# Cosformer attention and squared-ReLU MLP: the sequence tails become one more batch in seven products, the squares get three half buffers, and the casts of v move to GpSimd

## The chip, the cores and the metric

The kernel runs on one core of a Trainium2 chip, in one launch. The metric is the device time of that core in microseconds (us). Of the kernel before there are three timed runs and one profiled execution.

## The reference

```python
def _attn_ref(q, k, v):                       # q, k, v: (8, 8, 576, 64) float32
    theta = np.pi / 2.0 * np.arange(S) / S    # S = 576
    def phi(x, c, s):
        r = np.maximum(x, 0.0)
        return np.concatenate([r * c, r * s], axis=-1)
    q_p, k_p = phi(q, cos_w, sin_w), phi(k, cos_w, sin_w)
    kv = np.einsum('bhsf,bhsd->bhfd', k_p, v)
    z = np.sum(k_p, axis=2)
    num = np.einsum('bhsf,bhfd->bhsd', q_p, kv)
    den = np.einsum('bhsf,bhf->bhs', q_p, z)[..., None] + 1e-06
    return (num / den).astype(np.float32)

def _moe_ref(x, w_in, w_out):                 # x: the attention's output as (4608, 512)
    r = np.maximum(x @ w_in, 0.0)             # w_in: (512, 2048)
    return ((r * r) @ w_out).astype(np.float32)   # w_out: (2048, 512)
```

## The kernel before, in words

**Tiling.** The unit of work is one of the eight batches, with 576 positions: 512 main positions and a tail of 64. For each batch there is an attention part (features of k and q, casts of v, the small products `kz` and `num`, the division, transposes) and an MLP part on 512 tokens: a first matmul (`x @ w_in`, ReLU, square into `gT`) and a second one (`gT @ w_out`). The tails of four batches together make one more block of 256 tokens: tails of batches 0 to 3, and of 4 to 7.

**Plain and seven products.** Batches 0 to 2 do the first matmul plainly (`declare_plain`, lines 712 to 742: 16 blocks of eight matmuls with 256 columns each). Batches 3 to 7 (`SEVEN`, line 259) use a scheme with seven block products in the place of eight (`declare_seven1`, lines 810 to 872): four rounds of seven products of four matmuls, that is 112 matmuls for 512 tokens where the plain form takes 128. The price is sums: four differences of x per batch on VectorE (`declare_x_sums`, line 796), three copies per round on ScalarE, and per round two `add_relu` (line 421) on VectorE. The second matmul uses seven products in batches 1 to 7 (`declare_pair`, line 922): per pair of 128-token tiles, four sums of `gT` into `gs1` to `gs4` on VectorE (line 936), then Q1 to Q7 with eight matmuls each.

**The tails.** `declare_tails` (lines 746 to 769) makes the first matmul of a block of tails plainly, as eight pieces of eight matmuls: 64 per block, 128 in all. Lines 1236 to 1240 place the pieces: those of block 0 in batches 3, 4 and 5 (3, 3 and 2 pieces), those of block 1 in batches 6 and 7 (3 and 5 pieces). The second matmul of a block is a pair of its own (pair 2) in the middle of batches 5 and 7. `gTt` holds the squares of a block.

**Squares.** `gT` (line 311) is one buffer for the squares of 512 tokens. A square of the next batch can only be written when both pairs of the running batch have read that part; in rounds 0 to 2 one VectorE instruction squares all 512 tokens of two row blocks (line 870), in round 3 there are two halves (line 865).

**Casts.** `declare_v` (line 520) casts v to bf16 into `vx`. `declare_att` (line 1031) gives these casts to ScalarE for batches 3 to 7, to either of ScalarE and VectorE for batches 1 and 2. `vx` has five buffers; the cast of the next batch takes the buffers that `kz` (line 535) of the batch before has read. The load of v of the batch after has one buffer and waits for the casts.

**The order of the work.** Nothing is left to a scheduler at run time. Every operation is declared with the engines that may do it, an assumed cost, and for TensorE a position; `Planner.plan` (line 128) puts them into one fixed order for each engine, and the table `SHIFTS` (line 21) moves single operations, by their number, in it. All engines run their lists in order and wait on semaphores. So a changed list of operations gives a new order on all engines. SyncE's queue carries the loads of batches 0 and 3 to 7, all DMA transposes and the stores of batches 1 to 7; GpSimd's queue carries the weights, the loads of batches 1 and 2 and the two stores of batch 0 (`st_name`, line 876).

Of the kernel before, what the change touches and what calls it, by code (L numbers as in the profile page):

```python
# [20 lines left out]
SHIFTS = """  # L21
23:9.5:ACT 37:-0.5 38:1.0 44:17.5:ACT 46:-1.0 53:-0.5 62:11.5 79:-2.0 85:-2.5 89:3.0 93:11.0
108:5.5 144:9.0 152:-2.0 157:9.5:ACT 191:-5.0 194:-1.0 202:-1.5 203:-3.5:ACT 204:2.0 210:3.0
238:2.5 241:2.5 243:5.0 249:-6.0 257:-4.0 260:-2.0 261:-6.0 270:2.5 271:3.5 287:-5.0 325:-2.0
335:-0.5 340:1.5 348:8.5 354:-7.0 364:-19.0 383:1.0 390:-3.5 392:1.0 417:-4.5 487:-5.0 492:1.5
516:-7.5 517:-5.5 530:39.0 533:25.5 546:9.0 563:5.5 565:12.5 573:-8.5 575:5.0 588:13.0 593:4.5
598:-2.0 611:-4.5 617:-5.5 636:-1.5 670:7.5 677:-2.0 690:1.0 698:0.0:DVE 702:22.5 703:-19.5
704:3.5:ACT 706:-4.0 715:2.0 731:-2.5 748:5.0 781:-4.5 783:-6.0 785:-7.0 787:-2.0 790:-1.0
794:-1.5 797:1.0 799:1.0 807:11.0 813:-5.5 817:-4.0 820:-7.0 822:-5.5 836:-3.5 850:-3.5
859:-34.0 860:-15.0 870:1.0 872:-4.0 884:12.0 890:49.0 893:17.0 906:5.5 907:23.5 911:3.0 917:3.0  # L30
936:-3.0 951:-12.5 957:-1.0 958:-1.5 963:-3.5 985:7.0 990:-4.0 998:3.5 1005:-4.5 1009:5.5
1023:-10.0 1024:-8.5 1030:-10.0 1041:-26.0:ACT 1042:-10.5 1133:-13.0 1143:1.5 1155:4.0 1157:3.0
1176:-4.5 1191:4.5 1209:5.5 1247:2.5 1306:-0.5
# [200 lines left out]
def kernel(  # L234
# [24 lines left out]
    SEVEN = range(3, B)  # L259

# [7 lines left out]
        "round": 3, "rs": 6, "rt": 2, "u": 6, "gTt": 1, "ysb": 2,  # L268
        "gs1": 1, "gs2": 1, "gs3": 1, "gs4": 1,
# [7 lines left out]
    def many(pool, shape, dt=BF16):  # L277
# [29 lines left out]
        "gTt": many("gTt", [HB, 4 * TAIL]),  # L307
        **{f"gs{n}": many(f"gs{n}", [HBH, P]) for n in range(1, 5)},
        "ysb": many("ysb", [2, DM], F32),
    }  # L310
    gT = big.tile([P, HB, MAIN], BF16, name="gT")
# [126 lines left out]
    plan = Planner(POOLS, 4.5, ("gs1", "gs2", "gs3", "gs4"), 1.0, SHIFTS)  # L438
# [3 lines left out]
    TAILN = {3: 3, 4: 3, 5: 2, 6: 3, 7: 5}  # L442
    g1_len = {b: (7 if b in SEVEN else 8) * 16 * T_MM + TAILN.get(b, 0) * PROD2 for b in range(B)}
    g2_len = {b: 7 * PROD2 * (3 if b in (5, 7) else 2) if b else 8 * 2 * PROD2 for b in range(B)}
    att_len = 2.4
    T1, T2, t = {}, {}, 16.4
    for b in range(B):
        T1[b], T2[b] = t, t + g1_len[b] + att_len / 2
        t = T2[b] + g2_len[b] + att_len / 2

    loaded, kpb, vxb, kvzb, qpb, qpTb, xb, xTb, xTtb = ({} for _ in range(9))
# [68 lines left out]
    def declare_v(b, j, engs):  # L520
        buf = cached(vxb, (b, j), "vx" if j < J else "vxt")
        n = 1 if j < J else 0.65
        cost = {"ACT": 0.52 * n, "DVE": 0.34 * n}

        def cast(eng):
            copy(eng, at(buf)[:, :, 0:D], piece("v", b, j))

        add({e: cost[e] for e in engs}, cast, r=[source("v", b, j)], w=[buf])

    def declare_kz(b, pos, engs=("ACT",)):  # L530
        ba, bb = plan.buf("F"), plan.buf("F")
        kvz = kvzb[b] = plan.buf("kvz")
        for j in range(NS):

            def kz(_, j=j):
# [18 lines left out]
                ("PE", T_MM65 * (2 if j < J else 1) * HH + 0.02),  # L554
# [50 lines left out]
    def declare_num(b, j, pos):  # L605
# [22 lines left out]
        add(("PE", T_MM65 * n * HH + 0.015), num, r=[qT, kvzb[b]], w=bks, pos=pos)  # L628
# [76 lines left out]
    def gkey(hb, half):  # L705
        return ("g", hb // 2, half)
# [5 lines left out]
    def declare_plain(b, hb, half, pos, split=False):  # L712
# [3 lines left out]
        for c in range(2) if split else (None,):  # L716
# [23 lines left out]
            lambda _: square(gT[:, hb : hb + 2, half * TP : (half + 1) * TP], at(rt)),  # L740
            r=[rt], w=[gkey(hb, half)],
        )

    gttb, turned = {}, {}

    def declare_tails(b, hb, pos):

        bk, rt = plan.buf("F"), plan.buf("rt")
        xT = xTt_of(b)
        gt = cached(gttb, b // 4, "gTt")  # L750

        def tails(_):
            for i in range(2):
                for kb in range(KB):
                    mm(
                        bank(bk)[:, i * TP : (i + 1) * TP].rearrange("p (m c) -> p m c", m=4),
                        w1_at(kb, hb + i),
                        at(xT)[:, :, kb % 2, kb // 2, :],
                        i == 0 and kb == 0,
                        kb == KB - 1,  # L760
                    )

        add(("PE", PROD2), tails, r=[(xT, m) for m in range(4)] + [("w1", hb // 4)], w=[bk], pos=pos)
        add(("ACT", 0.5), lambda _: relu(at(rt), bank(bk).rearrange("p (i c) -> p i c", i=2)), r=[bk], w=[rt])
        add(
            ("DVE", 0.34),
            lambda _: square(at(gt)[:, hb : hb + 2, :], at(rt)),
            r=[rt], w=[(gt, hb // 2)],
        )
# [26 lines left out]
    def declare_x_sums(b):  # L796
        buf = xsb[b] = plan.buf("xs")
        x0, x1 = xT_of(b, 0), xT_of(b, 1)
        a = lambda kk, half: at((x0, x1)[half])[:, kk * KB2 : (kk + 1) * KB2, :]
        t = lambda n: a(0, 1) if n == 3 else at(buf)[:, min(n, 3) - 1]  # L800
        xk = [[(x0, 0), (x0, 1)], [(x1, 0), (x1, 1)]]
        for n, ops, reads in (
            (1, lambda: (a(0, 1), a(0, 0)), xk[0] + xk[1]),
            (2, lambda: (a(1, 1), t(1)), xk[1] + [(buf, 1)]),
            (3, lambda: (a(1, 1), a(0, 1)), xk[1]),
            (4, lambda: (a(1, 0), t(2)), xk[0] + [(buf, 2)]),
        ):
            add(("DVE", 0.34), lambda _, n=n, ops=ops: sub(t(n), *ops()), r=reads, w=[(buf, n)] + (xk[1] if n == 3 else []))

    def declare_seven1(b, r, t):  # L810
# [4 lines left out]
        xs, x0, x1 = xsb[b], xT_of(b, 0), xT_of(b, 1)  # L815
        xk = [[(x0, 0), (x0, 1)], [(x1, 0), (x1, 1)]]
        X = lambda kk, half: at((x0, x1)[half])[:, kk * KB2 : (kk + 1) * KB2, :]
        Tn = lambda n: X(0, 1) if n == 3 else at(xs)[:, min(n, 3) - 1]
        halves = lambda ap: ap.rearrange("p (i c) -> p i c", i=2)
        block = lambda i, j: at(rows[i])[:, :, j * TP : (j + 1) * TP]  # L820
        last = r == 3

        def product(name, off, acc, w, x, first, reads):
            def seven(_):
                for i in range(2):
                    for kb in range(KB2):
                        mm(
                            bank(acc)[:, i * TP : (i + 1) * TP],
                            w()[:, kb, i * P : (i + 1) * P],
                            x()[:, kb, :],  # L830
# [20 lines left out]
            ("DVE", 0.63), lambda _: add_relu(block(1, 1), halves(bank(E)), halves(at(u3))),  # L851
# [4 lines left out]
            ("DVE", 0.63), lambda _: add_relu(block(0, 1), halves(bank(E)), halves(at(u2))),  # L856
            r=[E, u2], w=[(rows[0], 1)],
        )
        for i in range(2):
            hb = i * HBH + 2 * r  # L860
            if last:
                for j in range(2):
                    add(
                        ("DVE", 0.34),
                        lambda _, i=i, j=j, hb=hb: square(gT[:, hb : hb + 2, j * TP : (j + 1) * TP], block(i, j)),
                        r=[(rows[i], j), turn], w=[gkey(hb, j)],
                    )
            else:
                add(
                    ("DVE", 0.6), lambda _, i=i, hb=hb: square(gT[:, hb : hb + 2, :], at(rows[i])),  # L870
                    r=[(rows[i], 0), (rows[i], 1), turn], w=[gkey(hb, 0), gkey(hb, 1)],
# [4 lines left out]
    def st_name(b):  # L876
        return "SP" if b >= 1 else "POOL"

    def st_eng(b):
        return nc.sync if b >= 1 else nc.gpsimd  # L880
# [24 lines left out]
    def four(b):  # L905
        return 0 if b < 7 else 1

    def g_at(b, pair, i, j):
        if pair == 2:
# [432 lines left out]
```

## Time and profile before

| what | value |
|---|---|
| timed runs | 276.74, 278.27, 279.21 us (median 278.27) |
| profiled execution: time, span | 276.82 us, 274.8 us |
| TensorE matmul busy | 267.9 us (98% of the span), 2845 matmuls |
| VectorE, ScalarE, GpSimd busy | 218.9, 194.9, 21.6 us |
| first wait for `w_in` after which TensorE runs without long gaps | until 22.19 us |
| last matmul starts, the span ends | 271.06 us, 274.8 us |

A page of the profile has the busy time of each engine, a strip of 40 slices (tenths of a slice that an engine was busy), the chain of work that ended last, and the costliest groups of instructions. Further answers of the trace are lists in order of time and tables of busy time by stretch. A matmul's recorded duration [...]overlaps with the next; the time from one start to the next is what it costs when TensorE is full. The same goes, less strongly, for VectorE and ScalarE.

### The profile page before, as it was taken

How to read it: one execution, taken by the hardware profiler on the slowest of the kernel's cores; microseconds unless marked ns; L12 is line 12 of the kernel's file. 1: busy time of each engine (PE TensorE's matmuls, PEld its weight loads, DVE VectorE, ACT ScalarE, POOL GpSimd, SP SyncE). 2: the span in 40 equal slices, each digit the busy share in tenths (PEclk: the TensorE clock that was granted, in tenths of full speed). 3: DMA queues.
4: the chain of work that ended last, by engine and by line, in shares of the span. 5: the costliest groups of instructions: out<-in, count | busy, mean ns of one | idle time of the engine just before them, and what ended most of it. 6: DMA issues, size and time to landing. Idle time of an engine off the chain costs nothing.

```text
span 274.8 us, 7115 instructions
## 1 busy us (share of the span) xinstructions
PE 267.9 (98%) x2845; PEld 227.6 (83%) x2845; DVE 218.9 (80%) x515; ACT 194.9 (71%) x391; POOL 21.6 (8%) x38
## 2 busy tenths in 40 slices
PE   8979999999999999999999999999999999999994
PEld 3668856789988988888888898988988888888884
DVE  1789996997694989699968999799968798279652
ACT  3876982997895598589957994699735954684522
POOL 1453544010000000000000000000000000000000
PEclk9999999999999999999999999999999999999999
DMA  7999999969979998899299955996198301200025
GB/s 217 321 205 290 296 283 365 219 218 225 361 160 186 281 334 156 224 347 221 81 164 308 259 181 102 265 338 217 35 205 170 91 2 44 95 16 2 1 79 153
DMA packets 81840, 53.01 MB, mean 193 GB/s; under 512 B 53584, under 2 KB 77648, under 8 KB 81808
## 3 DMA queue, kind: packets, MB, share of 16 engines
q1 hardware_dynamic: 75136, 40.12, 58.4%
q0 software_dynamic: 6528, 12.32, 17.1%
q8 instruction: 22, 0.36, 0.5%
q10 hardware_dynamic: 144, 0.13, 0.1%
q14 instruction: 10, 0.08, 0.1%
HBM read 36.70 MB, written 9.44 MB: 168 GB/s over the span
## 4 chain that ended last, share of the span: by engine, by line
PE 80%; DMA 8%; DVE 7%; issue 1%; SPq 1%; POOL 1%; ACT 1%; DVEq 0%
PE banks L430 79%; DMA w1sb<-in_moe_w_in_dram 4%; DMA qpT<-qp 2%; DMA vt<-in_v_dram 2%; DVE rs L422 2%; DVE gT L419 2%; DVE gs L427 2%; PE banks L591 1%; DVE x L639 1%; POOL w1sb L373 1%; SPq L366 0%; PE banks L682 0%; DVE qp L408 0%; DVE kp L408 0%; SPq L358 0%
## 5 line engine op out<-in xcount | busy, mean ns | idle before, releaser
L430 PEld LDWEIGHTS <-w1sb 128*128 128x128 bf16 x784 | 73.0, 98 | 10.4 <-DMA w1sb<-in_moe_w_in_dram 1.4
L430 PE MATMUL banks<-xT,w1sb 128*128 128x256 bf16 (+1 forms) x576 | 68.4, 267 | 1.0 <-DMA w1sb<-in_moe_w_in_dram 1.0
L430 PEld LDWEIGHTS <-gs 128*128 128x128 bf16 x512 | 49.0, 98 | 5.9 <-DVE gs L427 0.2
L416 ACT ACTIVATE rt<-banks 128x512 bf16<-128x512 f32 x64 | 37.2, 600 | 14.9 <-PE banks L430 9.3
L430 PEld LDWEIGHTS <-gT 128*128 128x128 bf16 x400 | 38.0, 98 | 9.0
L430 PE MATMUL banks<-w2sb,gT 128*128 128x256 bf16 (+1 forms) x288 | 44.2, 296 | 0.0
L430 PEld LDWEIGHTS <-w1s 128*128 128x128 bf16 x320 | 30.7, 98 | 3.7
L430 PE MATMUL banks<-w2sb,gs 128*128 128x256 bf16 x256 | 33.0, 273 | 0.0
L430 PE MATMUL banks<-w2s,gs 128*128 128x256 bf16 x256 | 32.2, 273 | 0.0
L422 DVE CUSTOM_DVE_ANT_0 rs<-banks,sums 128x512 bf16<-128x512 f32 x40 | 27.0, 684 | 4.5 <-ACT sums L847 3.1
L419 DVE TENSOR_TENSOR gT<-rs 128x1024 bf16<-128x1024 bf16 (+1 forms) x50 | 27.7, 579 | 1.8 <-ACT rs L416 1.0
L416 ACT ACTIVATE rs<-banks 128x512 bf16<-128x512 f32 x40 | 23.6, 604 | 3.1 <-PE banks L430 2.9
L430 PE MATMUL banks<-xs,w1s 128*128 128x256 bf16 x160 | 23.0, 273 | 0.0
L430 PE MATMUL banks<-xT,w1s 128*128 128x256 bf16 x160 | 22.9, 273 | 0.0
L419 DVE TENSOR_TENSOR gT<-rt 128x512 bf16<-128x512 bf16 x48 | 19.2, 418 | 4.5 <-ACT rt L416 4.3
L427 DVE TENSOR_TENSOR ysb<-banks,sums 128x256 f32<-128x256 f32 x32 | 13.4, 418 | 11.2 <-PE banks L430 7.3
L406 ACT ACTIVATE qp<-q,sin_col 128x512 bf16<-128x512 f32 x31 | 22.1, 738 | 0.1
L639 DVE TENSOR_TENSOR x<-banks,den 128x512 bf16<-128x512 f32 x30 | 20.7, 691 | 1.0
L406 ACT ACTIVATE kp<-k,sin_col 128x512 bf16<-128x512 f32 x30 | 21.2, 734 | 0.0
L427 DVE TENSOR_TENSOR gs<-gT 128x1024 bf16<-128x1024 bf16 x28 | 19.2, 686 | 1.1 <-PE banks L430 0.7
L413 ACT CAST vx<-v 128x512 bf16<-128x512 f32 x26 | 16.2, 636 | 0.9 <-DMA v<-in_v_dram 0.9
L637 DVE TENSOR_SCALAR den<-banks 128x8 f32<-128x8 f32 (+1 forms) x38 | 6.0, 159 | 12.5 <-PE banks L430 12.3
(106 smaller groups left out, 364.0 us busy)
## 6 DMA issues: line engine op xcount, KB each, us to landing
out_dram<-ysb SPq DMA_DIRECT2D x13, 512.0 KB, 3.5
k<-in_k_dram SPq DMA_DIRECT2D x6, 1024.0 KB, 6.4
v<-in_v_dram SPq DMA_DIRECT2D x5, 1024.0 KB, 7.9
q<-in_q_dram SPq DMA_DIRECT2D x5, 1024.0 KB, 9.3
w1sb<-in_moe_w_in_dram POOLq DMA_DIRECT2D x4, 512.0 KB, 10.5
q<-in_q_dram POOLq DMA_DIRECT2D x2, 1024.0 KB, 11.2
w2sb<-in_moe_w_out_dram POOLq DMA_DIRECT2D x4, 512.0 KB, 11.6
k<-in_k_dram POOLq DMA_DIRECT2D x2, 1024.0 KB, 11.3
```

The lines of the kernel that those rows point to most:

```text
L373: nc.gpsimd.dma_start(out=w1sb[:, :, f0:f1], in_=moe_w_in[:, f0:f1].rearrange("(kb p) f -> p kb f", p=P),)
L406: nc.scalar.activation(out=dst, in_=src, func=ACTF.Relu, scale=col)
L413: (nc.scalar.copy if eng == "ACT" else nc.vector.tensor_copy)(out=out, in_=in_)
L416: nc.scalar.activation(out=out, in_=in_, func=ACTF.Relu)
L419: nc.vector.tensor_tensor(out=out, in0=in_, in1=in_, op=ALU.mult)
L422: nc.vector._custom_dve(TENSOR_ADD_SAT, out=out, in0=in0, in1=in1, s0=float("inf"), s1=0.0)
L427: nc.vector.tensor_tensor(out=out, in0=in0, in1=in1, op=op)
L430: nc.tensor.matmul(out=out, lhsT=lhsT, rhs=rhs, start=start, stop=stop, skip_group_check=True)
L591: nc.tensor.transpose(t[:, h, :], qp_at(b, j)[:, h, :], ident[:, :])
L637: nc.vector.tensor_single_scalar(out=d, in_=n4[:, :, :, D], scalar=EPS, op=ALU.add)
L639: nc.vector.tensor_tensor(out=x_at(b, j).rearrange("p (b k) (l d) -> p b k l d", b=n, l=2), in0=n4[:, :, :, 0:D].rearrange("p b (k l) d -> ...
```

## The change

The tails of all eight batches become one more batch of 512 tokens, called `ENDS`, behind batch 6 and ahead of batch 7. Its first matmul is made in seven products, with the two blocks of tails as its two halves, so it has x sums, round copies and `add_relu` like the others; its second matmul is two pairs. `declare_tails`, `gTt` and the pairs 2 are gone. The squares go into three half buffers of 256 tokens (pool `gT`), which `claim` hands out in turn, so that the next batch can write into the third half and into the first one that comes free. The first product rounds are placed 3 to 6 us ahead (`LEAD`), among the second matmul of the batch before. The casts of v of batches 2 to 7 go to GpSimd as `tensor_scalar` (multiply by 1 twice). The cosine features of q may go to ScalarE or VectorE. The two stores of batch 0 go from GpSimd's to SyncE's queue. Assumed costs and `SHIFTS` are new, and with them the order on every engine.

```diff
+    ENDS = B
+    STAGES = [*range(B - 1), ENDS, B - 1]
...
-        "round": 3, "rs": 6, "rt": 2, "u": 6, "gTt": 1, "ysb": 2,
-        "gs1": 1, "gs2": 1, "gs3": 1, "gs4": 1,
+        "round": 3, "rs": 6, "rt": 2, "u": 6, "ysb": 2,
+        "gs1": 1, "gs2": 1, "gs3": 1, "gs4": 1, "gT": 3,
...
-        "gTt": many("gTt", [HB, 4 * TAIL]),
+        "gT": many("gT", [HB, TP]),
...
-    gT = big.tile([P, HB, MAIN], BF16, name="gT")
...
+    LEAD = [0,0,0,3,6,6,6,6,6]
...
+            if eng == "POOL":
+                nc.gpsimd.tensor_scalar(
+                    out=at(buf)[:, :, 0:D], in0=piece("v", b, j), scalar1=1.0, scalar2=1.0, op0=ALU.mult, op1=ALU.mult
+                )
...
+    def claim(b):
+
+        for half in range(2):
+            gh[b, half] = plan.buf("gT")
+            given([gh[b, half]], 0.0, lat=0.0)
...
+    def x_halves(b):
...
+        x = [xTt_of(half * 4) for half in range(2)]
+        return (
+            lambda kk, half: at(x[half])[:, :, :, kk, :].rearrange("p m k c -> p k m c"),
+            [[(x[half], m) for m in range(4)] for half in range(2)],
+        )
...
-    def declare_tails(b, hb, pos):
...
+                def squares(_, i=i, hb=hb):
+                    i0, i1 = sorted(gh[b, j].i for j in range(2))
+                    square(
+                        mem["gT"][:, i0 : i1 + 1 : i1 - i0, hb : hb + 2, :],
+                        at(rows[i]).rearrange("p k (s c) -> p s k c", s=2),
+                    )
...
     def st_name(b):
-        return "SP" if b >= 1 else "POOL"
+        return "SP" if b >= 0 else "POOL"
...
-    def declare_att(b, kpos, npos, cos_k=BOTH, cos_q=DVE1, cast=ACT1):
+    def declare_att(b, kpos, npos, cos_k=BOTH, cos_q=BOTH, cast=("POOL",)):
...
-    TAILS = {b: [] for b in range(B)}
-    TAILS[3], TAILS[4], TAILS[5] = [(3, 0, 3)], [(3, 3, 3)], [(3, 6, 2)]
-    TAILS[6], TAILS[7] = [(7, 0, 3)], [(7, 3, 5)]
-    PAIRS = {b: [0, 1] for b in range(B)}
-    PAIRS[5], PAIRS[7] = [0, 2, 1], [0, 2, 1]
...
-    for b in range(2, B):
+    for b in STAGES[2:]:
         if b > 2:
-            if b in SEVEN:
+            claim(b)
+            if b in SEVEN or b == ENDS:
                 declare_x_sums(b)
                 for r in range(4):
-                    t = T1[b] + r * 7 * PROD1
+                    lead = LEAD[STAGES.index(b)]
+                    t = T1[b] - lead + r * (7 * PROD1 + lead / 4)
                     declare_seven1(b, r, t)
-            for m, first, n in TAILS[b]:
-                for i in range(first, first + n):
-                    declare_tails(m, 2 * i, T2[b] - 1.5 + 0.01 * i)
...
-        for i, pair in enumerate(PAIRS[b]):
-            declare_pair(b, pair, T2[b] + i * 7 * PROD2)
+        for pair in range(2):
+            declare_pair(b, pair, T2[b] + pair * 7 * PROD2)
```

How the new order differs, counted in instructions: TensorE has 16 matmuls fewer (2845 before, 2829 after), all of them with 256 columns. VectorE goes from 515 instructions to 499, ScalarE from 391 to 387; GpSimd gets 30 casts (24 of 128x512, 6 of 128x256).

## The prediction

> **What bounds the kernel now.** I read the page's head and strips first, then the table of stretches, then the list in order of time at the place where one matmul hands over to the next.
>
> ```profile
> span 274.8 us, 7115 instructions
> PE 267.9 (98%) x2845; PEld 227.6 (83%) x2845; DVE 218.9 (80%) x515; ACT 194.9 (71%) x391; POOL 21.6 (8%) x38
> PE   8979999999999999999999999999999999999994
> PEclk9999999999999999999999999999999999999999
> PE 80%; DMA 8%; DVE 7%; issue 1%; SPq 1%; POOL 1%; ACT 1%; DVEq 0%
> ```
>
> TensorE is full from the third slice to the last but one at full clock, and 80% of the chain that ended last is its own. A busy TensorE need not be at its peak, so I take the time from start to start:
>
> ```profile
> 130.42 0.69 DVE L427 TENSOR_TENSOR gs<-gT 128x1024 bf16<-128x1024 bf16 x1
> ...
> 131.15 0.69 DVE L427 TENSOR_TENSOR gs<-gs,gT 128x1024 bf16<-128x1024 bf16 x1
> ...
> 131.35 1.91 PE L430 MATMUL banks<-w2s,gs 128*128 128x256 bf16 x16
> ...
> 131.75 0.68 DVE L422 CUSTOM_DVE_ANT_0 rs<-banks,sums 128x512 bf16<-128x512 f32 x1
> ...
> 133.10 0.41 PE L430 MATMUL banks<-vx,kp 128*128 128x65 bf16 x8
> ```
>
> Columns: start, us, engine, line, operation. Sixteen matmuls from 131.35 to 133.10 are 1.75 us, 109 ns each, though one is recorded as 273 ns. Summed over all matmuls by such steps (109 ns for 256 columns, 29.5 for 65, 216 for 512, 55 for 128), the trace has 260.3 us of streaming between first and last start (1.19 and 271.06). The rest is 9.6 us: some 5.8 before 22.2 us (start, waits for w_in), 2.5 in steps of 0.09 to 0.10 us to and from 64-row tail products in every batch, which the change keeps, and only some 1.3 in real waits: 0.56 at 123.7 to 124.2 (for a ScalarE copy behind VectorE work), 0.36 at 143.3 (a transpose of qp), 0.19 at 99.0, crumbs. So the bound is the number of columns streamed. The fence also shows how tight the cover is: gs1 ends at 131.11, its matmul starts at 131.35.
>
> ```profile
> core 0: us, PE busy (x) PEld busy (x) DVE busy (x) ACT busy (x) POOL busy (x), PEclk, DMA share, GB/s
> 116.50:145.60 29.10, 28.56 (x310) 25.25 (x309) 25.91 (x59) 24.15 (x51) 0.00 (x0) 1.00 0.86 202
> 176.00:210.00 34.00, 34.00 (x375) 30.45 (x374) 30.32 (x69) 24.26 (x52) 0.00 (x0) 1.00 0.81 207
> 210.00:238.00 28.00, 28.00 (x269) 24.92 (x268) 21.13 (x44) 17.06 (x36) 0.00 (x0) 1.00 0.26 61
> ```
>
> With attention in a stage VectorE is at 89% and loses 0.5 us for TensorE in one of them; the late stages, without attention, have 25% to spare. GpSimd does nothing there.
>
> **What the Trainium skill says.** "TensorE: Matmul & The Clock Gate", section Back-to-back issue gap: 262 cycles at 2.4 GHz for 256 columns, 109 ns; the trace agrees. "Perfetto Trace Analysis", section Identifying the Most-Contended Engine: matmul busy time is no measure of distance to the roofline; hence the steps above. "SBUF — State Buffer", section Who interferes with whom: a GpSimd instruction that reads SBUF and a VectorE instruction with two SBUF inputs, or in a two-port mode, shut each other out for the whole instruction. No run here shows it yet; GpSimd computes nothing after 9 us before. "GPSIMD Engine Reference", section 3.1: 512 elements at about 1.8 cycles take 769 ns, the best body 1.03 cycles.
>
> **The change, part by part.**
>
> *Tails in seven products.* Removed: 16 pieces of 8 matmuls, 128. Added: 4 rounds of 7 products of 4, 112. The second matmul keeps 2 x 56. So 16 x 0.109 = **-1.74 us**. The tail matmuls of before (group of banks from xTt and w1sb, x128) have the same 273 ns as the others with the same strided right side, so no price for that. VectorE: out 16 squares of 0.335 (5.4), in 8 add_relu of 0.60 (4.8), 6 squares of 0.60 and 4 of 0.335 (4.9), 4 x sums of 0.335 (1.3), all start to start: +5.6 us. ScalarE: out 16 ReLUs of 0.48, in 12 copies and 8 ReLUs of 0.48: +1.9 us. Both lie in a stage without attention, whose TensorE length is 224 x 0.109 = 24.4 us against VectorE's 22.1 - 4.9 = 17.2 (ledger below): hidden. Uncovered they would cost 5.6.
>
> *Tails gone from batches 3 to 5.* There they were filler, 3 x 0.87 = 2.6 us per stage. Ledger of a middle stage on VectorE: x sums 1.3, add_relu 4.8, squares 4.9, gs sums 8 x 0.605 = 4.8, y 4 x 0.334 = 1.3, divisions 4 x 1.03 + 0.74 = 4.9; 22.1 us, and cosine features up to 3.7 more. TensorE: 224 x 0.109 + 80 x 0.0295 + 0.38 = 27.2. By the new order VectorE keeps 2 to 7 of 10 cosine features of batches 5 to 7, 0.8 to 2.6 us (before: nearly all of q's), so it has 22.9 to 24.7 of 27.2. ScalarE: 12 copies and 8 ReLUs 9.6, pairs 10 x 0.26, sine features 5.7, kvz 0.5, and the cosines up to 5.7 less VectorE's share: 22 to 23. Room of 2.5 to 4.3 us on VectorE, as before (3.2 of 29.1): no cost.
>
> *Casts on GpSimd.* 21 casts of 0.51 and 4 of 0.30 leave ScalarE, 5 leave VectorE. They get longer on GpSimd, but vx has a whole stage until its kz: the latency is hidden. What isn't known is the blocking. Each cast can hold a VectorE sum or square back by at most its own length, 0.44 to 0.77 us by the skill's rates plus dispatch; four and a tail per stage are at most 3.5 us, about all the room. Where they fall: four wait for vx to be freed by kz, and the new order has kz of batches 5 and 6 directly ahead of Q1, so the casts of 6 and 7 run exactly beside the last squares, gs1 and gs2. The slack there is a few tenths (0.24 above). I take 0.3 us at each of two such places, **+0.6**; bounds 0 (lock taken beside PSUM reads) and 12 casts x 0.77 = 9 for the three batches freed by kz.
>
> *Half buffers and mixing.* Before, squares of rounds 0 to 2 wait until both pairs have read gT; after, until pair 0 has. No instruction more: 36 squares in place of 30 are the extra stage. Product rounds of the next batch were already mixed in; more of them stand at the handover. I count that half of the 1.3 us of waits goes, **-0.6**; bounds -1.3 and 0. The cover is more rounds' worth of banks; gone, the 1.3 stays.
>
> *Stores of batch 0 on SyncE.* They were issued at 52.37 and 55.54; on SyncE they now stand ahead of the first transpose of qp, which started at 51.14. It can go some 5 us later; the first product that needs qpT starts at 71.8. Two issues of 0.5. Hidden. Behind it on that queue the loads of batch 3 follow, which have 20 us.
>
> *Start.* One product piece of the first matmul stands behind the second weight chunk, a num ahead of it: 0.44 against 0.24 us; and four transposes (0.22) come earlier. Nothing, -0.2 to +0.5.
>
> *End.* Same last pair, same 3.7 us after the last matmul's start.
>
> Sum: -1.74 + 0.6 - 0.6 = -1.74. Against the profiled execution, 274.8 span and 2.0 around it: 276.82 - 1.74 = 275.1. The median of the runs shown, 278.27, is 1.45 above that execution; so 276.5.
>
> **The rivals.**
>
> *Casts bind (slower).* Place: squares, gs1 and gs2 at the handovers of batches 2 to 4. If the 12 casts behind kz each cost TensorE 0.5 us, 6 us: 276.82 - 1.74 - 0.6 + 6 + 1.45 = 281.9. It decides from (1.74 + 0.6)/12 = 0.2 us per cast. For it: the 0.24 us of slack, and that by the groups some two thirds of VectorE's busy time has two SBUF inputs or is a scaled copy within SBUF. Against: TensorE's order has the next batch's products to set between.
>
> *Filler gone (no change).* The tails were what TensorE did while VectorE was full from 113.85 to 140. Without them the middle stages lose what the product count wins, 3 stages x 0.6: 278.3. Against: the room of the ledger.
>
> *All waits go (faster).* -1.74 - 1.3 - 0.2 = -3.2: 275.0. For it: casts off ScalarE, squares less bunched. Against: the lock.
>
> That the change doesn't remove what it says is no rival: the 16 matmuls are gone from the list.
>
> **How the numbers follow.** Forecast 50%, own range 275.2 to 277.8; all waits go 22%; no change 15%; casts bind 13%. One per cent, about what a measurement of this kernel can tell from no change (its three runs lie 0.9% apart), is 2.8 us: faster below 275.5, slower above 281.05. Faster: most of the third case and a fifth of the first, 0.31; slower: most of the last, 0.10; within: 0.59. The range for 8 in 10, 273.9 to 279.6, has the second and third case and the milder half of the casts.
>
> **What would show it.** Right: 2829 matmuls, last one starting near 269.3; no gap above 0.3 us after 22 us; VectorE near 215 us plus any lengthening. Wrong: casts far over 0.8 us, squares or gs sums recorded well over 0.68 us or starting late beside casts, gaps of TensorE at gs1; idle TensorE in batches 3 to 5 with VectorE full; a late first qpT. A start past 23 us would make it wrong for another reason.

## The result, and the profile after

The changed kernel takes 279.52 us (median of 20 runs, 277.63 to 281.31); the kernel before, beside it on the same chip, 277.53 us (20 runs, 276.74 to 279.92). The ratio is 1.0058, 95% interval 1.0035 to 1.0081: slower by 0.6%, some 1.6 us, where 1.7 us less was forecast. (The ratio is that of the means; the medians lie 2.0 us apart.) Every ratio below is to runs of the kernel before on the chip of that run.

The head of the page, TensorE's strip, the chain that ended last, and the group of the new casts:

```profile
span 277.1 us, 7122 instructions
...
PE 267.5 (97%) x2825; PEld 224.9 (81%) x2829; DVE 219.3 (79%) x499; ACT 196.4 (71%) x387; POOL 41.0 (15%) x66
...
PE   8879999999999999999999999999999999999994
...
PE 66%; DVE 17%; DMA 10%; issue 2%; SPq 2%; ACT 1%; POOL 1%; DVEq 0%
...
L530 POOL TENSOR_SCALAR vx<-v 128x512 bf16<-128x512 f32 x24 | 17.2, 744 | 85.9 <-DMA v<-in_v_dram 85.9
```

The span is 2.3 us longer. The strip looks as full as before, so it can't tell the cause. The chain can: TensorE's share falls from 80% to 66%, VectorE's rises from 7% to 17%. Counted as in the prediction, from start to start, streaming fell from 260.3 to 258.6 us (four 512-column records that the trace lacks are added), as forecast; waits and other gaps rose from 9.6 to 13.4; the part after the last matmul's start by 0.3. -1.75 + 3.8 + 0.3 is the 2.3 of the span. By stretch the gaps (all time from one matmul's start to the next that is more than its columns take) are:

| TensorE's gaps, us | up to 25 us | 25 to 95 | 95 to 135 | 135 to 225 | 225 to the end |
|---|---|---|---|---|---|
| before | 5.8 | 1.0 | 1.3 | 1.4 | 0.1 |
| after | 6.6 | 1.1 | 2.9 | 2.1 | 0.8 |

The largest growth, 1.6 us, lies between 95 and 135 us, at the handovers of batches 2 and 3 to their successors. VectorE in order of time there, in the changed kernel:

```profile
117.84 0.35 DVE L410 TENSOR_SCALAR kpt<-kt,cos_col 128x256 bf16<-128x256 f32 x1 [0.89 <-DMA kt<-in_k_dram]
118.11 0.68 DVE L424 CUSTOM_DVE_ANT_0 rs<-banks,sums 128x512 bf16<-128x512 f32 x1
...
126.33 0.83 DVE L410 TENSOR_SCALAR kp<-k,cos_col 128x512 bf16<-128x512 f32 x1
127.08 0.82 DVE L421 TENSOR_TENSOR gT<-rs 128x512 bf16<-128x512 bf16 x1
127.82 0.62 DVE L410 TENSOR_SCALAR kp<-k,cos_col 128x512 bf16<-128x512 f32 x1
```

and TensorE's first matmuls after its two waits there:

```profile
118.85 0.60 PE L432 MATMUL banks<-xT,w1s 128*128 128x256 bf16 x4 [0.44 <-DVE rs L424]
...
129.82 0.61 PE L432 MATMUL banks<-w2sb,gT 128*128 128x256 bf16 x4 [0.39 <-DVE gT L421]
```

Columns: start, us, engine, line, operation; in brackets the idle time before it and what ended it. Two things show. A feature of batch 5's tail (attention runs ahead of the MLP) stood in VectorE's list ahead of a row sum and waited 0.89 us for its load; TensorE waited for that row sum. And beside the casts, which ran from 124.56 to 128.2 us, features that take 0.48 us elsewhere took 0.62 and 0.83, and a square that takes 0.42 took 0.82. Over the whole trace 12 VectorE instructions beside casts are longer than their own kind by 0.14 to 0.42 us, 3.4 us together (called lengthening below); in the kernel before, GpSimd computes nothing after 9 us.

### The profile page after: what moved, and what is told of

The parts are those of the page before. It is cut to its first block, busy times and chain, and to the rows that moved or that the text cites. A ratio compares the mean times of both kernels' runs of the same rounds, so it can differ in the third digit from the quotient of the medians.

```text
span 277.1 us, 7122 instructions
## 1 busy us (share of the span) xinstructions
PE 267.5 (97%) x2825; PEld 224.9 (81%) x2829; DVE 219.3 (79%) x499; ACT 196.4 (71%) x387; POOL 41.0 (15%) x66
## 2 busy tenths in 40 slices
DMA packets 81842, 53.03 MB, mean 191 GB/s; under 512 B 53584, under 2 KB 77648, under 8 KB 81808
## 4 chain that ended last, share of the span: by engine, by line
PE 66%; DVE 17%; DMA 10%; issue 2%; SPq 2%; ACT 1%; POOL 1%; DVEq 0%
PE banks L432 65%; DVE gT L421 5%; DVE rs L424 4%; DMA w1sb<-in_moe_w_in_dram 4%; DMA k<-in_k_dram 3%; DVE gs L429 2%; DMA vt<-in_v_dram 2%; DVE kp L410 1%; DMA kt<-in_k_dram 1%; DVE x L647 1%; SPq L368 1%; DVE den L646 1%; PE banks L599 1%; SPq L360 1%; PE banks L690 0%
## 5 line engine op out<-in xcount | busy, mean ns | idle before, releaser
L432 PEld LDWEIGHTS <-w1sb 128*128 128x128 bf16 x704 | 65.0, 98 | 9.2 <-DMA w1sb<-in_moe_w_in_dram 1.3
L432 PEld LDWEIGHTS <-gT 128*128 128x128 bf16 x448 | 42.6, 98 | 10.3 <-DVE gT L421 0.7
L432 PEld LDWEIGHTS <-w1s 128*128 128x128 bf16 x384 | 36.7, 98 | 6.0 <-issue 1.2
L424 DVE CUSTOM_DVE_ANT_0 rs<-banks,sums 128x512 bf16<-128x512 f32 x48 | 32.6, 684 | 7.0 <-PE banks L432 4.2
L418 ACT ACTIVATE rt<-banks 128x512 bf16<-128x512 f32 x48 | 27.6, 596 | 13.9 <-PE banks L432 8.0
L421 DVE TENSOR_TENSOR gT<-rs 128x1024 bf16<-128x1024 bf16 (+1 forms) x60 | 34.7, 601 | 2.6 <-ACT rs L418 1.9
L418 ACT ACTIVATE rs<-banks 128x512 bf16<-128x512 f32 x48 | 28.2, 603 | 5.0 <-PE banks L432 4.4
L530 POOL TENSOR_SCALAR vx<-v 128x512 bf16<-128x512 f32 x24 | 17.2, 744 | 85.9 <-DMA v<-in_v_dram 85.9
L432 PE MATMUL banks<-xs,w1s 128*128 128x256 bf16 x192 | 27.4, 273 | 0.0
L429 DVE TENSOR_TENSOR ysb<-banks,sums 128x256 f32<-128x256 f32 x32 | 13.4, 420 | 6.9 <-ACT sums L977 3.7
L857 ACT COPY sums<-banks 128x512 f32<-128x512 f32 x24 | 14.2, 592 | 5.2 <-PE banks L432 5.0
```

The lines of the kernel that those rows point to most:

```text
L418: nc.scalar.activation(out=out, in_=in_, func=ACTF.Relu)
L421: nc.vector.tensor_tensor(out=out, in0=in_, in1=in_, op=ALU.mult)
L424: nc.vector._custom_dve(TENSOR_ADD_SAT, out=out, in0=in0, in1=in1, s0=float("inf"), s1=0.0)
L429: nc.vector.tensor_tensor(out=out, in0=in0, in1=in1, op=op)
L432: nc.tensor.matmul(out=out, lhsT=lhsT, rhs=rhs, start=start, stop=stop, skip_group_check=True)
L530: nc.gpsimd.tensor_scalar(out=at(buf)[:, :, 0:D], in0=piece("v", b, j), scalar1=1.0, scalar2=1.0, op0=ALU.mult, op1=ALU.mult)
```

## The experiments

Four theories: the casts hold VectorE up (the hold); the order puts waiting instructions in front of what TensorE needs; the start is later because `w2` and k are loaded earlier; the tails are missing as filler. Unless an order is moved by name below, the planned order of all engines stays.

**The changed kernel again**, unedited.

> The changed kernel as it is, once more, so that the experiments have it on their own chip beside the kernel before. Every theory expects what was measured first: 1.0035 to 1.0081 of the kernel before, VectorE instructions longer by about 3.4 us beside the casts.

1.0048 (1.0029 to 1.0067); 3.6 us of lengthening. The result stands, at 1.005.

**Short casts.**

```diff
-                    out=at(buf)[:, :, 0:D], in0=piece("v", b, j), scalar1=1.0, ...
+                    out=at(buf)[:, :, 0:8], in0=piece("v", b, j)[:, :, 0:8], scalar1=1.0, ...
```

> The changed kernel with its order of instructions untouched, and each cast on GpSimd cut from 64 to 8 of the 64 columns of a head: the other 56 columns of v are left out of the result. The changed kernel is at 1.0058 of the kernel before, some 1.6 us behind, and 12 VectorE instructions beside its casts are longer by 3.4 us together. If the casts' hold on VectorE is the cause of the loss, most of it comes back: 1.000 of the kernel before or less, with the stalls at 127.9 and 129.8 us gone. If the loss comes from the order in which VectorE and ScalarE take features that wait for loads, from the start, or from the tails that no longer fill gaps, the stalls at 101.7 and 118.9 us stay and the time is 1.004 to 1.006.

0.9955 (0.9932 to 0.9978): 0.9% better than the changed kernel, and better than the kernel before. The casts are the larger part of the loss. The waits at 101.7, 118.9 and 127.9 us stayed (0.73, 0.41 and 0.32 us), so something of the order remains; the wait at 129.8 us is gone, and gaps in 95 to 225 us fell by 1.4 us. No VectorE instruction beside the short casts is longer by 0.04 us or more.

**Short casts with the hold put back.** Are casts costly because they hold VectorE, or because they are ready late?

```diff
+                own = at(source("v", b, j)).bitcast(BF16)
+                nc.gpsimd.tensor_scalar(
+                    out=(own[:, :, j, 0:56] if j < J else own[:, :, 0:56]), in0=piece("v", b, j)[:, :, 8:64],
...
```

> The short casts of e1 (8 of 64 columns, the rest of v left out), and behind each a second GpSimd instruction that casts the other 56 columns into the used part of v's own buffer, which no one reads. What TensorE needs is there as early as with the short casts, but GpSimd is as long on the memory as with complete casts, about 0.73 us for both and 0.58 for one complete cast. If the casts cost by holding VectorE up, the whole loss is back: 1.004 to 1.008, VectorE instructions lengthened by 3 us or more. If they cost by being ready late, the time stays where the short casts put it: 0.994 to 0.998.

1.0040 (1.0013 to 1.0067), gaps 13.4 us as in the changed kernel, 2.4 us of lengthening (3 or more were expected). The same two instructions of VectorE's list at 95 us (start, us, line, operation), in the changed kernel, with short casts, and with the hold put back:

```profile
95.70 1.10 DVE L429 TENSOR_TENSOR gs<-gT,gs 128x1024 bf16<-128x1024 bf16 x1
96.72 0.82 DVE L421 TENSOR_TENSOR gT<-rt 128x512 bf16<-128x512 bf16 x1
```

```profile
95.08 0.69 DVE L429 TENSOR_TENSOR gs<-gT,gs 128x1024 bf16<-128x1024 bf16 x1
95.68 0.46 DVE L421 TENSOR_TENSOR gT<-rt 128x512 bf16<-128x512 bf16 x1
```

```profile
95.66 1.04 DVE L429 TENSOR_TENSOR gs<-gT,gs 128x1024 bf16<-128x1024 bf16 x1
96.62 0.45 DVE L421 TENSOR_TENSOR gT<-rt 128x512 bf16<-128x512 bf16 x1
```

The sum gs is long where GpSimd works beside it for long, and at its own 0.69 us where it does not. By its making the run does not rule lateness out, against what was expected: only the first of a batch's four casts is as early as with short casts, and the fourth ends here at 98.75 us, in the changed kernel at 98.61. What rules it out is the list of waits: here, in the changed kernel, in its repeat and in the run that comes next, no wait of any engine ends with a GpSimd cast. So it is the hold. (The runs with short casts and with the hold put back were on different chips, as were the two of the pair that follows; each ratio is to the kernel before on its own chip.)

**The casts alone, in the kernel before**: `declare_v` there emits the same `tensor_scalar` on GpSimd for batches 2 to 7.

> The kernel before with its order untouched, and the casts of v of batches 2 to 7 run by GpSimd at the places of the order where ScalarE ran them; tails and buffers as before. ScalarE is relieved of some 16 us. If the casts' hold on VectorE is the cause of the loss, this one part alone makes the kernel before slower by 1.5 to 3 us: 1.005 to 1.011, with VectorE instructions longer by 3 us or so beside the casts. If the hold is of no account, the relieved ScalarE keeps it level or makes it faster: 0.997 to 1.002.

1.0048 (1.0030 to 1.0065), with 4.0 us of lengthening, on the same chip as the repeat of the changed kernel. This one part alone makes the kernel before as slow as the whole change does, although ScalarE's busy time falls from 194.9 to 185.2 us. (26 of the 30 casts were ScalarE's and four VectorE's there, so it is some 10 us and not the 16 of the expectation.)

**Short casts in the kernel before**: the same, with 8 columns.

> The kernel before, order untouched, with the casts of v of batches 2 to 7 on GpSimd and cut to 8 of 64 columns (the other columns of v are left out of the result): ScalarE relieved of some 16 us, and next to no hold on VectorE; tails and buffers as before. It answers to the short casts in the changed kernel (0.9955), with everything else of the change left out. If the tails' seven products, the half buffers and the mixing are worth the 1.7 us of TensorE that they save, it stands that much behind: 1.000 to 1.003. If they are worth nothing on the clock, because the tails' matmuls had filled waits, the two are level: 0.994 to 0.997.

0.9965 (0.9945 to 0.9985). Two readings. Against complete casts in the same order, 0.8% or 2.3 us is the hold. Against the kernel before, -0.35% or 1.0 us is what taking the casts from ScalarE and VectorE is worth here. And against short casts in the changed kernel (0.9955) there is no difference that can be measured: -0.1%, with an uncertainty of 0.3. All the rest of the change together is worth nothing that shows, although 1.7 us of matmuls are gone. What that rest is made of isn't separated: with short casts ScalarE is busy for 195.7 us in the changed kernel and 185.4 here, because it also got cosine features and the tails' round copies.

**Each cast twice.**

> The changed kernel with its order untouched, and each cast on GpSimd made twice in a row, the second time over the first with the same values, so that the result is complete. Short casts stand at 0.9955, complete ones at 1.005. If the cost is the hold on VectorE and goes with GpSimd's time on the memory, as much again is added, 0.7 to 1.2%: 1.012 to 1.018, with VectorE lengthened by 6 to 7 us. If the cost was a single place that the first cast already hits, or the casts' place in the order, the second cast adds little: 1.004 to 1.008.

1.0274 (1.0244 to 1.0305), with 8.7 us of lengthening beside casts. That is more than either theory expected; what ended TensorE's waits says why:

```profile
PE banks L432 <- POOL vx L531: 3.3, 4, 1.2
```

(total us, times, longest). Now casts are ready too late as well, in four places; in the changed kernel no wait ends with a cast. The lengthening grows with GpSimd's work, but how much of the 2.2% is hold is not separated.

**The cast as a copy**: `nc.gpsimd.tensor_copy` in place of the multiplication.

> The changed kernel with its order untouched, and the casts on GpSimd written as a copy with a change of type in place of a multiplication by two ones. The result is complete. If the hold goes with the time that GpSimd is on the memory, and the copy is no faster than 0.62 us per cast, nothing changes: 1.003 to 1.007 of the kernel before, VectorE instructions lengthened by 3 us or more. If a plain copy is on the memory for less, or holds VectorE less, part of the 2.6 us comes back with a complete result: 0.997 to 1.001.

1.0068 (1.0048 to 1.0088); a cast takes 626 ns (median; 622 as multiplication), lengthening 3.4 us. Between these two forms of the cast no difference shows.

**The casts on ScalarE**, at the same places of the order.

> The changed kernel with its order untouched, and the casts of v for batches 2 to 7 run by ScalarE at the same places of the order, where GpSimd ran them. ScalarE gets 30 casts more, some 16 us of work. If the casts' hold on VectorE is the cause, the lengthened VectorE instructions are back at their 0.48 and 0.68 us, and the time falls to 1.002 or less even with the added ScalarE work. If the order at the handovers is the cause, the added ScalarE work comes at just these places, ahead of the copies that TensorE waits for, and the time rises: 1.008 to 1.02.

1.0356 (1.0308 to 1.0404). The lengthening is gone, yet the casts now stand in ScalarE's list ahead of copies that TensorE waits for (from 95 us on, 4.2 us in seven waits for a round's copies). This order was made for casts elsewhere; the run doesn't weigh ScalarE against GpSimd, it shows how little room a list has at the handovers.

**Waiting features moved back.** What the two expectations here call batches 3 and 4 are batches 4 and 5. A first version moved one ScalarE copy ahead of the product whose sums it reads, so part of the second product of batch 2 is formed from other data:

> The changed kernel with five instructions moved in their engines' orders and nothing else: the two features of kt of batch 4 (VectorE and ScalarE), which stood waiting for their load ahead of the row sums at 117.8 us, go behind those of the next two rounds; two features of k of batch 3 go behind the ScalarE copies of the second product that TensorE waited for at 101.7 and 104.0 us; one feature of k of batch 4 goes behind the copy it waited for at 127.9 us. If features that wait for loads in front of what TensorE needs are the cause in batches 2 and 3, the stalls of 0.64, 0.27 and 0.61 us at those places go and the end comes 1.0 to 1.5 us sooner: 1.001 to 1.002 of the kernel before. If the casts' hold on VectorE is the cause, VectorE is as late as ever at the next handover and the time stays at 1.005 to 1.006.

1.0054 (1.0029 to 1.0078), with a new wait of 1.48 us at 102.6 us; nothing follows from it. The second version moves each operation (left) behind one (right) that leaves it after what it reads:

```diff
+        for n, m in ((703, 648), (704, 656), (529, 580), (584, 583), (698, 675)):
+            op = next(o for o in order if o.n == n)
+            order.remove(op)
+            order.insert(1 + next(i for i, o in enumerate(order) if o.n == m), op)
```

> The changed kernel with five instructions moved in their engines' orders and nothing else, and each behind what it reads: the two features of kt of batch 4 go behind the row sums of the next rounds on VectorE and ScalarE; one feature of k of batch 3 goes behind the ScalarE copy that TensorE waited for at 101.7 us, and the copy waited for at 104.0 us goes ahead of one feature and one relu; one feature of k of batch 4 goes behind the copy waited for at 127.9 us. If features that wait for their loads in front of what TensorE needs are the cause in batches 2 and 3, the stalls of 0.64, 0.27 and 0.61 us there go, and the end comes 0.8 to 1.5 us sooner than the changed kernel's: 1.000 to 1.003 of the kernel before. If VectorE is simply full from 118 to 131 us, because of the casts' hold and without any lack in the order, the stalls move to the next handover and the time stays at 1.004 to 1.006.

1.0028 (1.0011 to 1.0045): 0.2% better than the changed kernel, less than the two intervals together. The waits at 101.7 and 118.9 us are gone, but a later one came:

```profile
123.99 0.60 PE L432 MATMUL banks<-xs,w1s 128*128 128x256 bf16 x4 [0.19 <-ACT banks L850]
127.02 0.60 PE L432 MATMUL banks<-xT,w1s 128*128 128x256 bf16 x4 [0.68 <-DVE rs L424]
```

A likely reason is in the table of stretches, from 118 to 131 us, for the changed kernel, with short casts, and for the kernel before:

```profile
core 0: us, PE busy (x) PEld busy (x) DVE busy (x) ACT busy (x) POOL busy (x), PEclk, DMA share, GB/s
118.00:131.00 13.00, 12.01 (x140) 10.03 (x138) 12.76 (x26) 12.10 (x24) 3.61 (x5) 1.00 1.22 284
```

```profile
118.00:131.00 13.00, 12.60 (x147) 10.91 (x147) 12.69 (x27) 12.49 (x25) 1.49 (x5) 1.00 1.00 307
```

```profile
118.00:131.00 13.00, 12.66 (x133) 11.19 (x131) 12.29 (x24) 12.14 (x26) 0.00 (x0) 1.00 1.06 280
```

VectorE is busy for 12.3 to 12.8 of the 13 us in all three (time in which an instruction is held counts as busy) and ScalarE for 12.1 to 12.5: what is late once has little room to catch up, and a wait taken away in one place comes back in the next. That it came back for this reason was not tried by itself.

**The load of w2 later.**

```diff
+            if op.n == 145:
+                nc.gpsimd.tensor_copy(out=w2sb[0:1, 0, 0:1], in_=w1sb[0:1, 0, 512:513])
```

> The changed kernel with one added GpSimd copy of one element that lets the load of the first quarter of w2, and all loads behind it on GpSimd's queue, wait for the second quarter of w1, as in the kernel before, where that load was issued at 19.1 us and not at 17.1. If the start lost its 0.7 us because w2 and k compete with the second quarter of w1, the matmul that waits for that quarter starts at about 19.6 us and not 20.3, and the end comes 0.5 to 0.8 us sooner: 1.003 to 1.004. If the start is late for another reason (the transposes and the batch 0 chain at 17.1 us), or if a later w2 then stalls the rows of batch 0 at 33 us, no change or slower: 1.006 or more.

1.0011 (0.9985 to 1.0037), but not for the reason given: the matmul that waits for the second quarter of w1 starts at 20.14 us, hardly earlier than the 20.33 of the changed kernel; in the unedited repeat it started at 20.04.

**Order and load together, complete casts**, and **all three edits with short casts**:

> The changed kernel, complete casts on GpSimd, with the five moved instructions and the later load of w2. If order and start are separate from the casts: 0.998 to 1.000 of the kernel before. If VectorE stays the bound through the casts' hold: 1.001 to 1.003, no better than the better of the two edits alone.

> The changed kernel with three edits at once: casts of 8 of 64 columns (the other columns of v are left out of the result), the five moved instructions, and the first load of w2 behind the second quarter of w1. Measured one by one against the kernel before: 0.9955, 1.0028 and 1.0011, where the changed kernel stands at 1.005. If the three losses are separate (2.6, 0.6 and 1.0 us), they add up: 0.988 to 0.992. If they are one loss seen three times, VectorE being late at the same handovers, no more than the casts' part comes back: 0.994 to 0.997.

1.0058 (1.0037 to 1.0079) and 0.9997 (0.9975 to 1.0020). The gains of the order and of the load do not add up, they vanish; neither is confirmed as a cause. Between the two, on one chip, short casts are worth 0.6%. Over the three comparisons (this one, 0.9% in the changed kernel, 0.8% in the kernel before) the hold costs 0.6 to 0.9%, that is 1.7 to 2.6 us.

**Less of the tails, in the kernel before.**

```diff
-                for kb in range(KB):
+                for kb in range(1):
...
-                        kb == KB - 1,
+                        True,
```

> The kernel before with its order untouched, and each of the 16 first products of the tails cut from 8 matmuls to 2, so that only the first quarter of the sum over DM is formed for the tails; VectorE's and ScalarE's work on them stays. 96 matmuls of 0.109 us are gone, 10.5 us of TensorE. If the tails filled nothing, all of it comes off the end: 267 us, 0.962 of the kernel before. If their 2.6 us per batch were the cover that VectorE's chains need at the handovers, so that their going cost the changed kernel its gain, 1 to 3 us come back as waits of TensorE in batches 3 to 5: 0.966 to 0.973.

1.0019 (0.9997 to 1.0041). 10.5 us of matmuls are gone and nothing is gained: gaps rose from 9.6 to 20.6 us, of which 6.9 lie in 135 to 225 us and 4.2 at the end. What ended TensorE's waits between 95 and 270 us:

```profile
PE banks L430 <- DVE rs L422: 2.4, 5, 0.8
PE banks L430 <- ACT rt L416: 1.3, 3, 0.7
PE banks L430 <- ACT sums L847: 1.3, 4, 0.5
PE banks L430 <- DVE gs L427: 1.0, 3, 0.6
```

In the kernel before the same list is two waits, 0.3 and 0.2 us. In this order these matmuls cost nothing: they filled time in which the rounds' copies, row sums and sums were not ready.

**The same with the casts on GpSimd.**

> The kernel before with both earlier edits: the tails' first products cut from 8 matmuls to 2 (only the first quarter of the sum over DM is formed for the tails), and the casts of v of batches 2 to 7 on GpSimd. Alone, the casts cost 0.48% with the tails' matmuls in place, and the short tails 0.19%. If the tails cover VectorE's lateness, so that a hold on VectorE reaches TensorE in full without them, the casts now cost more, about as in the changed kernel: 1.010 to 1.014. If the two have nothing to do with each other, the sum: 1.006 to 1.008.

1.0062 (1.0036 to 1.0089), the mere sum. That the tails also cover the hold is not borne out.

**Shorter sums of gT**, in the changed kernel and in the kernel before with short tails:

```diff
-... sub(at(gs[n]), *ops(), op)
+... sub(at(gs[n])[:, 0:2], *(x[:, 0:2] for x in ops()), op)
```

> The changed kernel with its order untouched, and each of VectorE's four sums of gT ahead of a second product formed for 2 of 8 blocks only (the rest of the sums is left at zero, so that the result is another): 0.69 us become about 0.2 us, 56 times, and VectorE has some 27 us less to do, spread over the handovers. If TensorE's waits between 95 and 270 us, some 6 us, are VectorE being late at the handovers, for whatever reason, 3 to 5 us of them go: 0.987 to 0.994 of the kernel before. If they come from loads, transposes or ScalarE, they stay: 1.003 to 1.006.

> The kernel before with the tails' first products cut from 8 matmuls to 2 (a quarter of the sum over DM) and with VectorE's sums of gT formed for 2 of 8 blocks only, the rest at zero. The short tails alone took 10.5 us of matmuls away and gained nothing (1.0019). If what then held the end was VectorE at the handovers, the shorter sums let the saving through: 0.965 to 0.980. If the saving was lost to something else (loads, transposes, the places of the order), the time stays at 0.995 to 1.002.

0.9988 (0.9967 to 1.0010) and 0.9848 (0.9812 to 0.9883). Both gain, 0.6% and 1.7% against the same kernel with whole sums, both less than expected. The second stands 4.2 us under the kernel before, of the 10.5 us that were taken out; how much of that the shorter sums would gain with the tails' matmuls in place was not run. Then this ends TensorE's waits:

```profile
PE banks L430 <- ACT sums L847: 2.4, 4, 1.4
PE banks L430 <- DVE rs L422: 1.6, 4, 0.6
```

The sums' waits are gone and ScalarE's copies within a round take their place. By these waits it isn't VectorE's amount of work alone; it is the chain of a round, over ScalarE and VectorE, in an order made for the full matmuls.

**No cast by an engine from batch 3 on: v loaded as bf16** into vx, four loads and two for the tail per batch.

```diff
+                nc.gpsimd.dma_start(out=vx_at(b, j)[:, :, 0:D], in_=v[b, :, 0:MAIN, :].rearrange("h (p j) d -> p h j d", j=J)[:, :, j, :])
```

> The changed kernel with its order, but from batch 3 on no engine casts v: GpSimd's queue loads v as bf16 straight into the buffers that the products read, in four loads and two for the tail, at the places where SyncE loaded v as f32. The result is complete. If the casts' hold on VectorE is the cause, and writing the loads' descriptors does not hold VectorE in the same way, the time comes near to that of the short casts: 0.995 to 0.999 of the kernel before. If loads in pieces of 64 columns are slow enough to make v or the transposes late, or if their issue on GpSimd holds VectorE too, nothing is gained: 1.004 to 1.015.

1.0473 (1.0417 to 1.0530). Of the lengthening 0.8 us is left, beside the casts of batch 2, but packets under 512 B rose from 53584 to 74304, and the transposes of qp came late, landing 7.6 us after their issue where it was 4.5 (medians; the page, and the waits of TensorE):

```profile
DMA packets 97441, 50.07 MB, mean 171 GB/s; under 512 B 74304, under 2 KB 93248, under 8 KB 97408
```

```profile
PE banks L432 <- DMA qpT<-qp: 9.0, 2, 4.7
```

That the small packets made the transposes late is not shown. A part of the loss is the clock: 42 matmuls of 256 columns took some 0.21 us to the next start and not 0.109, most of them in slices of the page where 0.7 to 0.8 of the clock was granted, some 4 us together; the kernel before has one such step.

No version with a complete result beat the kernel before.

## Why the prediction was wrong

*Tails in seven products, -1.74.* The streaming fell by 1.7 us, as worked out. That this comes off the end is the step that failed first. I had read the kernel before as bound by the columns streamed, because only 1.3 us were real waits. But a list that is full of filler has no waits to see: in the kernel before 96 of these 128 matmuls could be taken out for nothing. With the casts' hold nearly out of both kernels, what is left of the change stands at -0.1% (0.3 either way), where -2.3 us, or 0.8%, was forecast. In the trace with short casts the 1.7 us went into gaps: 1.0 us more than before in 95 to 135 us, 0.65 at the last handovers, 0.2 at the start, and 0.1 less in between. That those at 95 to 135 us stand there for want of filler, and not through the new order itself, is argued from the kernel before and not shown in the changed one.

*Tails gone from batches 3 to 5: no cost.* Wrong, with the same root. The ledger had set VectorE's sum of work against TensorE's and found 2.5 to 4.3 us of room in each stage. The short tails took 1.3 to 2.0 us out of each stage of batches 3 to 6, 11 pieces of 6 matmuls, 7.2 us; 6.5 us of gaps came back between 95 and 225 us. The sum over a stage is not the test; in the kernel before VectorE is busy for 12.3 of 13 us at a handover, and for 25.9 of 29.1 over the stage around it. The rival "filler gone" had this right for the kernel before, and its price, what the product count wins, is about what was found.

*Casts on GpSimd, +0.6.* Right in kind, mis-sized: 1.7 to 2.6 us. I put it at two places, the handovers ahead of batches 6 and 7. The lengthened instructions lie at six places from 52 to 182 us, one for each batch whose v is cast there. The Trainium skill, "SBUF — State Buffer", section Who interferes with whom, says that one engine shuts the other out for the whole instruction, and the traces agree (last section): a held instruction loses what is left of the cast, 0.45 us at most here. So "casts bind" named the mechanism, at 0.5 us for each of 12 casts too high a price. The relief of ScalarE, 1.0 us by the short casts in the kernel before, was not in my sum; it stands against the hold. In the changed kernel ScalarE is not less busy in the end (196.4 us, 194.9 before).

*Half buffers and mixing, -0.6.* Not seen. Real waits did not halve; gaps grew by 3.8 us. Of the growth, 0.65 us is at the last handovers (232 to 266 us), where no cast runs, and much the same in every run of the changed kernel but that with shorter sums (0.4). Why VectorE is late there was not tried.

*Start, 0; end, 0.* The start took 6.6 us of gaps against 5.8, in the repeat 6.1; two runs of the kernel before with other casts have 6.3 and 6.8, so it is mostly variation between executions. The end was 0.3 us longer, a small miss that returns in the repeat. *Stores of batch 0: hidden.* As forecast: the first transpose of qp starts at 54.4 us and not 51.1, and the first product that reads it at 71.9 as before.

So the loss adds up like this, from the same runs and not from an independent measurement: casts off ScalarE and VectorE -1.0, hold +1.7 to 2.6, the rest -0.3 (0.8 either way); that is 0.4 to 1.3, with the same 0.8 either way, against 1.3 to 1.6 measured. What stays open is what the rest consists of, and why the later w2 and the moved features gained 0.2 to 0.4% alone and nothing together.

## What to carry to other kernels

Before booking matmuls that are to be saved, take some of them out where they stand and see whether the end moves: in a fixed order without visible waits they may be filler, worth nothing. Judge cover by the full stretch at a handover, not by an engine's sum over a stage. Work moved to GpSimd isn't free for VectorE even if no one waits for its result; look for VectorE instructions that are longer than their own kind.

## What the runs showed of the hardware

Which VectorE instructions the casts held was sharper than expected. In five executions with complete casts (the changed kernel, its repeat, the moved features in their second version, the later w2, and the casts alone in the kernel before), 86 instructions with all their large operands in SBUF (squares, sums of gT, features) overlapped a cast by more than 0.15 us, and 58 of them were longer by more than 0.04 us, up to 0.45. Of 102 that read PSUM, or only a few columns (row sums, divisions, copies from banks), none was. The Trainium skill, "SBUF — State Buffer", section Who interferes with whom, says this of instructions with at most one SBUF input outside the two-port modes, and the traces agree. The casts pay too: 0.62 us undisturbed, up to 1.16 beside such an instruction.

How they wait for each other can be read from the ends. The first two casts beside the sum gs and the square gT of the changed kernel that are shown above (95.70 and 96.72 us):

```profile
95.48 0.79 POOL L530 TENSOR_SCALAR vx<-v 128x512 bf16<-128x512 f32 x1 [17.96 <-DMA v<-in_v_dram]
96.23 1.05 POOL L530 TENSOR_SCALAR vx<-v 128x512 bf16<-128x512 f32 x1
```

The first cast ends at 96.27 us and the sum, due 0.4 us sooner, at 96.80, 0.53 later. The second cast ends at 97.28, 0.48 after the sum, and the square at 97.55, 0.27 after that cast. All 58 lengthened instructions end like this, whenever they began: those of 1024 columns 0.53 to 0.54 us after the end of a cast, squares of 512 columns 0.27 to 0.31 after it, features of 512 columns 0.28 (the one feature of 256 columns 0.14). And the casts of 512 columns that are longer by over 0.04 us end 0.47 to 0.48 us after the end of a VectorE instruction whose large operands all lie in SBUF. So the two don't share and slow down. One stands still until the other is done, and what it loses is what was left of the other.
